# Re-timing three small visits in a fused attention and FFN kernel: a v product joined to its scores, a value pair moved ahead, and four k transposes given to the DMA queue

## The chip, the cores and the metric

The kernel runs on one core of one Trainium2 chip. The metric is device time in microseconds (us) of one execution, lower is better. Each timed comparison runs the changed kernel and the kernel before on the same chip, in rounds; ratios with 95% intervals come from those.

Before the change the median was 402.93 us (three runs, 402.53 to 404.41).

## The reference

```python
# 8 batches, 8 heads, 1024 positions, head size 64; E, F: 64 x 1024
k_proj = einsum('ks,bhsd->bhkd', E, k)
v_proj = einsum('ks,bhsd->bhkd', F, v)
attn   = softmax(q @ k_proj^T / sqrt(64))          # over 64 projected keys
x      = (attn @ v_proj), heads side by side        # 8192 x 512
h      = max(x @ w1, x @ w2, x @ w3)                # 512 -> 768, three times
out    = h @ w_out                                  # 768 -> 512
```

## The kernel before

The kernel does one batch of the FFN while it prepares the attention of the next one. TensorE (PE) works in program order. (A DMA *lands* when its data is complete at its destination.) The FFN products of batch b form a row of *steps*; a table, `plan(b)`, says which pieces of attention work ("visits") stand behind which step. Step `(ch, s)` is half `ch` of the batch; `s` from 0 to 5 are the up-projection steps (12 products of 128x512 each), 6 to 9 are output tiles (6 products each); `"mid"` means behind the eighth product of a step.

```python
# abridged; "..." marks cuts
def load(b, which):                       # q, k, v of one batch, 1 MiB each, POOL queue, cast to bf16
    for i in which:
        dma = nc.gpsimd.dma_start(out=tiles[i], in_=view((q, k, v)[i], b))
        if i == 0 and b - 1 in last_T:
            after(dma, last_T[b - 1])     # q of b waits for the DMA transpose of q of b-1

def qd(b, parts=1):                       # q: packed by DVE, turned by DMA into qTs[b]
    for lo in range(0, NPAIR, n):
        ...
        last_T[b] = nc.sync.dma_start_transpose(out=qTs[b][...], in_=q_p[...])

def kproj(b):                             # k product: 16 matmuls, then a copy to kps[b]
    ...
    copy("v", kps[b]..., t[:, 0:4 * D], ns, 0.43)

def kt(b):                                # k turned by PE: two transposes into PSUM, one DVE copy
    t, ns = two()
    for gg in range(2):
        nc.tensor.transpose(out=t[:, gg * P:(gg + 1) * P], in_=kps[b][:, gg, :], identity=ident)
    kpTs[b] = att.tile([P, NPAIR, KP], BF16, name="kpT")
    copy("v", kpTs[b]..., t[:, 0:2 * P]..., ns, 0.3)

def vproj(b): ...                         # v product: 16 matmuls, four copies to vps[b]
def sc(b, g, ...): ...                    # scores of head pair g: needs qTs[b] and kpTs[b]; then exp
def zc(b, queue): ...                     # softmax sums, their inverse, zd to DRAM, zi broadcast back
def vx(b, g): ...                         # attention values of pair g, scaled by zi into x

def plan(b):
    if b == 0:
        return {
            (0, 7): [qd(1, 2), ...],      # q of batch 1 is turned in two halves
            ...
            (1, 0): [kproj(1)],
            (1, 1): [kt(1)],
            (1, 2): [vproj(1), ld(2)],
            (1, (3, "mid")): [sc(1, 0, now=True), sc(1, 1)],
            (1, 4): [za(1, 0), sc(1, 2, now=True)],
            ...
        }
    ...
    if b == 2:
        return {
            (0, 2): [kproj(3), vproj(3), ld(4)],
            (0, 3): [kt(3)],
            (0, 4): [sc(3, 0, now=True), sc(3, 1)],
            ...
            (0, 7): [zc(3)],
            (0, 8): [qd(4)],
            (1, 3): [kproj(4), vproj(4), ld(5), vx(3, 0), vx(3, 1)],
            (1, 4): [kt(4)],
            (1, 7): [vx(3, 2), vx(3, 3), sc(4, 0)],
        }
    ...                                   # batches 3 and later: one general row of visits

# start of batch 0: FFN products and attention visits are interleaved one by one
(0, 1, 3): [lambda: v_pair(2), lambda: x(2)],
(0, 1, 5): [lambda: v_pair(3), ld(1)],
```

The softmax here doesn't subtract the row's maximum and nothing guards it: scores larger than these inputs give would overflow.

## Time and profile before

| | before |
|---|---|
| time, median | 402.93 us |
| span of the profiled run | 400.4 us |
| PE busy | 388.4 us, 97% |
| VectorE (DVE) / ScalarE (ACT) busy | 203.5 / 151.0 us |

These are lines of parts 1, 2 and 3 of the page of the kernel before. Part 1 gives busy us, share of the span and instructions; the line of digits gives the busy share of the 16 DMA engines in tenths, in 40 slices.

```profile
span 400.4 us, 5708 instructions
PE 388.4 (97%) x2244; PEld 176.7 (44%) x2286; DVE 203.5 (51%) x319; ACT 151.0 (38%) x242; POOL 34.2 (9%) x49
DMA  9999999968799998999989959990890229020202
q0 software_dynamic: 29104, 30.41, 47.0%
```

PE is the limit, at 97%. But the digits of the DMA engines are 9 in most slices up to 270 us: a landing may come just in time, and then a later one costs.

This is the list of waits of the kernel before, PE only: who waited, for whom, us in total, how many times, the longest.

```profile
PE banks L461 <- DVE warm_f L175: 1.5, 1, 1.5
PE banks L346 <- DMA v_t<-in_v_dram: 1.0, 1, 1.0
PE banks L490 <- DMA k_t<-in_k_dram: 0.9, 1, 0.9
PE banks L232 <- DVE vp L102: 0.7, 2, 0.5
```

These are four of its ten lines; the others come to 2.7 us, none of their waits over 0.3. The 1.0 us is the wait that step 1 of the change is after, and one of the two waits of L232 is what step 2 is after. There is little else.

The timeline of the kernel before around that wait, PE lines (start, us from start to end, engine, line, operation, tiles, shape, count, and in brackets the idle time before it and what ended it):

```profile
52.15 2.75 PE L583 MATMUL banks<-xT,w_sb 128*128 128x512 bf16 x12
55.95 1.06 PE L346 MATMUL banks<-v_t,efT 128*64 128x256 bf16 x16 [1.04 <-DMA v_t<-in_v_dram]
56.94 1.90 PE L583 MATMUL banks<-xT,w_sb 128*128 128x512 bf16 x8
58.77 0.63 PE L212 MATMUL banks<-qT,kpT 64*64 64x512 bf16 x8
59.33 3.63 PE L583 MATMUL banks<-xT,w_sb 128*128 128x512 bf16 x15
```

Twelve products start 0.216 us apart, so those from 52.15 make room at 54.74; the v product starts at 55.95. And the timeline of the kernel before around the q load of batch 4 and the first scores of batch 4 (`sc(4, 0)`):

```profile
131.20 0.88 POOL L201 DMA_DIRECT2D q_t<-in_q_dram  x1 [24.63 <-DMA qT<-q_p]
168.22 0.63 PE L232 MATMUL banks<-pT,vp 64*64 64x512 bf16 x8
168.71 0.41 PE L212 MATMUL banks<-qT,kpT 64*64 64x512 bf16 x4
169.22 0.88 POOL L201 DMA_DIRECT2D q_t<-in_q_dram  x1 [35.40 <-DMA qT<-q_p]
```

The scores (L212) start without a listed wait, but the transpose of q that they read landed at 168.67: the q load of batch 5, which waits for exactly that landing, is issued at 169.22.

### The profile page before, as it was taken

The numbers are of one execution on the slowest core, as the hardware profiler recorded it, in microseconds if no ns is written. First come the engines' busy times: TensorE is split into PE (matmuls) and PEld (weight loads), VectorE is DVE, ScalarE is ACT, GpSimd is POOL, SyncE is SP. The second block draws the span as 40 slices with busy tenths as digits, with TensorE's granted clock in tenths as the row PEclk, the third lists the DMA queues.
The fourth block names the chain that finished last, engine by engine and source line by source line (L and its number), as shares of the span: only waits on it lengthen the run. The fifth ranks groups of instructions, "written<-read, shape, count | busy, mean of one in ns | idle before, by whom it ended". The sixth has DMA issues, their size and how long they took to land.

```text
span 400.4 us, 5708 instructions
## 1 busy us (share of the span) xinstructions
PE 388.4 (97%) x2244; PEld 176.7 (44%) x2286; DVE 203.5 (51%) x319; ACT 151.0 (38%) x242; POOL 34.2 (9%) x49
## 2 busy tenths in 40 slices
PE   7999989999999999999999999999999999999996
PEld 3444443353444445444454445444454444444443
DVE  2348746762683525736274544744267342745251
ACT  2535428527222462253323532245323533132312
POOL 7440002000400200010020000100000000000000
PEclk9999999999999999999999999999999999999999
DMA  9999999968799998999989959990890229020202
GB/s 159 205 206 208 230 204 156 235 137 156 203 187 198 221 218 193 223 183 209 224 221 178 236 133 269 178 242 26 204 217 5 103 67 252 0 105 2 105 0 105
DMA packets 66330, 66.09 MB, mean 165 GB/s; under 512 B 30624, under 2 KB 58784, under 8 KB 66304
## 3 DMA queue, kind: packets, MB, share of 16 engines
q0 software_dynamic: 29104, 30.41, 47.0%
q1 hardware_dynamic: 37056, 35.20, 34.3%
q8 instruction: 17, 0.28, 0.3%
q10 hardware_dynamic: 144, 0.13, 0.1%
q14 instruction: 9, 0.07, 0.1%
HBM read 69.73 MB, written 16.97 MB: 217 GB/s over the span
## 4 chain that ended last, share of the span: by engine, by line
PE 84%; DMA 9%; DVE 2%; issue 2%; ACT 1%; POOL 0%; DVEq 0%; ACTq 0%; POOLq 0%
PE banks L583 56%; PE banks L687 18%; DMA v_t<-in_v_dram 8%; PE banks L346 3%; PE banks L232 2%; PE banks L212 2%; DMA k_t<-in_k_dram 2%; DVE xT L309 1%; PE banks L257 1%; ACT zi_all L298 1%; ACT zl L292 1%; PE banks L490 1%; DVE m L652 0%; PE banks L461 0%; PE banks L516 0%
## 5 line engine op out<-in xcount | busy, mean ns | idle before, releaser
L583 PE MATMUL banks<-xT,w_sb 128*128 128x512 bf16 x1119 | 254.8, 379 | 2.6 <-issue 0.8
L583 PEld LDWEIGHTS <-w_sb 128*128 128x128 bf16 x1152 | 109.9, 98 | 136.1 <-issue 8.5
L652 DVE TENSOR_TENSOR m<-banks,h1s 128x512 f32<-128x512 f32 x90 | 62.1, 690 | 135.3 <-ACT h1s L648 92.7
L648 ACT COPY h1s<-banks 128x512 f32<-128x512 f32 x90 | 52.6, 585 | 120.3 <-PE banks L583 118.8
L687 PE MATMUL banks<-wout_sb,hT 128*128 128x512 bf16 x370 | 85.6, 379 | 1.0 <-issue 0.8
L593 DVE TENSOR_TENSOR hT<-banks,m 128x512 bf16<-128x512 f32 x90 | 62.3, 692 | 9.3
L687 PEld LDWEIGHTS <-hT 128*128 128x128 bf16 x378 | 35.2, 98 | 47.4 <-issue 5.6
L102 ACT COPY o_sb<-banks 128x512 f32<-128x512 f32 (+1 forms) x56 | 32.6, 582 | 57.9 <-PE banks L687 57.6
L223 ACT ACTIVATE pT<-banks 128x1024 bf16<-128x1024 f32 (+1 forms) x36 | 32.8, 932 | 18.1 <-PE banks L212 18.1
L309 DVE TENSOR_TENSOR xT<-banks,zi_all 128x1024 bf16<-128x1024 f32 x28 | 33.1, 1219 | 11.7 <-PE banks L232 6.9
L201 POOL DMA_DIRECT2D q_t<-in_q_dram x7 | 6.1, 878 | 193.8 <-DMA qT<-q_p 118.8
L346 PEld LDWEIGHTS <-efT 128*64 128x64 bf16 x224 | 11.6, 110 | 4.5 <-issue 3.0
L102 DVE CAST vp<-banks 64x256 bf16<-64x256 f32 (+1 forms) x18 | 7.1, 397 | 12.5 <-ACT vp L102 9.5
L102 ACT CAST vp<-banks 64x256 bf16<-64x256 f32 x14 | 5.1, 364 | 21.4 <-PE banks L346 21.3
L232 PE MATMUL banks<-pT,vp 64*64 64x512 bf16 (+1 forms) x144 | 11.4, 364 | 0.7 <-DVE vp L102 0.7
L212 PE MATMUL banks<-qT,kpT 64*64 64x512 bf16 (+1 forms) x144 | 11.4, 362 | 0.4 <-DVE m L652 0.3
L292 ACT ACTIVATE zl<-banks 128x512 f32<-128x512 f32 (+1 forms) x12 | 8.9, 739 | 6.3 <-PE banks L232 5.3
L102 DVE COPY q_p<-q_t 128x1024 bf16<-128x1024 bf16 x28 | 10.4, 435 | 0.5 <-DMA q_t<-in_q_dram 0.5
L346 PE MATMUL banks<-v_t,efT 128*64 128x256 bf16 x112 | 7.3, 273 | 1.0 <-DMA v_t<-in_v_dram 1.0
L102 DVE COPY o_sb<-banks 128x512 f32<-128x512 f32 (+1 forms) x9 | 5.8, 653 | 4.5 <-PE banks L667 4.5
L346 PE MATMUL banks<-k_t,efT 128*64 128x256 bf16 x112 | 7.4, 276 | 0.0
L461 PE MATMUL banks<-warm_f 128*128 128x512 f32 x8 | 6.0, 895 | 1.5 <-DVE warm_f L175 1.5
(63 smaller groups left out, 120.9 us busy)
## 6 DMA issues: line engine op xcount, KB each, us to landing
out_dram<-o_sb SPq DMA_DIRECT2D x30, 512.0 KB, 4.6
zi_all<-zd SPq DMA_DIRECT2D x20, 512.0 KB, 8.0
q_t<-in_q_dram POOLq DMA_DIRECT2D x7, 1024.0 KB, 10.1
k_t<-in_k_dram POOLq DMA_DIRECT2D x7, 1024.0 KB, 16.4
v_t<-in_v_dram POOLq DMA_DIRECT2D x7, 1024.0 KB, 21.9
zi_all<-zd POOLq DMA_DIRECT2D x4, 512.0 KB, 7.6
w_sb<-in_moe_w_dram POOLq DMA_DIRECT2D x4, 384.0 KB, 11.1
k_t<-in_k_dram POOLq DMA_DIRECT2D x2, 512.0 KB, 8.7
```

What stands on the lines that cost most here:

```text
L102: done = {"v": nc.vector.tensor_copy, "s": nc.scalar.copy, "g": nc.gpsimd.tensor_copy}[eng](out=o, in_=i)
L212: nc.tensor.matmul(out=t[c * HALF:(c + 1) * HALF, hp, 0:n * P], lhsT=kpTs[b][rows, g, :], rhs=qTs[b][rows, at:at + n, :], start=True, stop ...
L223: nc.scalar.activation(out=pTs[b, g, lo], in_=t, func=AF.Exp, scale=scale)
L232: nc.tensor.matmul(out=t[hp * HALF:(hp + 1) * HALF, c, 0:nsi * HALF], lhsT=w(rows, hp), rhs=p[rows, hp, :], start=True, stop=True,)
L292: nc.scalar.activation(out=zl, in_=t, func=AF.Ln)
L309: nc.vector.tensor_tensor(out=xTs[b][:, g, lo:lo + nsi, :].rearrange("a (c s) p -> a c (s p)", c=2), in0=t, in1=zi, op=ALU.mult,)
L346: nc.tensor.matmul(out=t[hh * HALF:(hh + 1) * HALF, 0:width], lhsT=efT[:, si, (kv - 1) * KP:kv * KP], rhs=qkv[b][kv][:, heads[hh], si, :], ...
L583: nc.tensor.matmul(out=h, lhsT=w_sb[i][:, ct, jt * P:(jt + 1) * P], rhs=xTs[b][:, ct, ch * SPC:(ch + 1) * SPC, :], start=(ct == first), st ...
L593: nc.vector.tensor_tensor(out=o, in0=h, in1=other, op=ALU.max)
L648: nc.scalar.copy(out=h1s, in_=h[0][0])
L652: nc.vector.tensor_tensor(out=m12, in0=h[1][0], in1=h1s, op=ALU.max)
L687: nc.tensor.matmul(out=o_ps, lhsT=hTs[b, ch][:, jt, tt * P:(tt + 1) * P], rhs=wout_sb[:, jt, :], start=(jt == 0), stop=(jt == NJT - 1),)
```

## The change

Three steps, each meant to take a PE wait or PE work away.

1. Batch 1's v product moves from behind step (1, 2), where PE waits for its load, into the visit of batch 1's first scores.
2. Value pair 2 of batch 0 moves two FFN products ahead, so that these fill the time in which its values are copied.
3. k of batches 3, 5, 6 and 7 is turned by a DMA transpose on SP's queue rather than by PE. The next batch's q load is made to wait for it.

```diff
@@ load
             if i == 0 and b - 1 in last_T:
                 after(dma, last_T[b - 1])
+            if i == 0 and b - 1 in turned:
+                after(dma, turned[b - 1])
@@ new
+    def kd(b):
+        def f():
+            kpTs[b] = att.tile([P, 2, 2 * KP], BF16, name="kpT2")
+            turned[b] = nc.sync.dma_start_transpose(
+                out=kpTs[b], in_=kps[b].rearrange("a g x -> a (g x)")
+            )
+        return f
@@ plan(0)
-                (1, 2): [vproj(1), ld(2)],
-                (1, (3, "mid")): [sc(1, 0, now=True), sc(1, 1)],
+                (1, (3, "mid")): [sc(1, 0, now=True), sc(1, 1), vproj(1), ld(2)],
@@ plan(2)
-                (0, 2): [kproj(3), vproj(3), ld(4)],
-                (0, 3): [kt(3)],
+                (0, 2): [kproj(3), kd(3), vproj(3), ld(4)],
@@ plan(3 and later)
-            out[1, 2] = [kproj(n + 1), vproj(n + 1)] + out[1, 2]
-            out[1, 3] = [kt(n + 1)]
+            out[1, 2] = [kproj(n + 1), kd(n + 1), vproj(n + 1)] + out[1, 2]
@@ start of batch 0
-                    (0, 1, 3): [lambda: v_pair(2), lambda: x(2)],
+                    (0, 1, 1): [lambda: v_pair(2)],
+                    (0, 1, 3): [lambda: x(2)],
```

(The scores read the new layout of `kpT` where a batch was turned by DMA; `turned` starts empty; `ld(n + 2)` stands alone at step (1, 3) now that `kt` has gone from there.)

More of the change, by code (lines that the diff above doesn't have):

```diff
@@ L203, in load, with k_pair @@
                 after(dma, last_T[b - 1])
+            if i == 0 and b - 1 in turned:
+                after(dma, turned[b - 1])
+    def k_pair(b, g):
+        if b in turned:
+            return kpTs[b][:, g % 2, (g // 2) * KP:(g // 2 + 1) * KP]
+        return kpTs[b][:, g, :]
+    turned = {}
     def scores(b, g, lo, nsi):
@@ L213, in scores @@
                     out=t[c * HALF:(c + 1) * HALF, hp, 0:n * P],
-                    lhsT=kpTs[b][rows, g, :],
+                    lhsT=k_pair(b, g)[rows],
                     rhs=qTs[b][rows, at:at + n, :],
@@ L758, in plan @@
             out[0, 4] = [qd(n + 1)]
-            out[1, 2] = [kproj(n + 1), vproj(n + 1)] + out[1, 2]
-            out[1, 3] = [kt(n + 1)]
+            out[1, 2] = [kproj(n + 1), kd(n + 1), vproj(n + 1)] + out[1, 2]
             out[1, 6] += [sc(n + 1, 0)]
         if n + 2 < B:
-            out[1, 3] += [ld(n + 2)]
+            out[1, 3] = [ld(n + 2)]
         return out
```

## The prediction

> **What bounds it now.** TensorE. Page part 1: matmuls busy 388.4 of 400.4 us, clock 1.0. The list of PE waits sums to about 8 us, mostly at the start. A 128x512 product starts every 0.216 us (timeline; 12 take 2.59). So a step pays only if it removes PE work or ends a PE wait; DMA matters only where a landing comes after PE's need.
>
> **Step 1, v product of batch 1.** In the timeline the product starts at 55.95 although the FFN products before it allow 54.74: a gap of 1.2 us for v_t, issued 25.64, landed 55.90. Moved behind the first scores, it no longer waits. But those scores then come at about 56.4, and the first half of qT(1) (DMA transpose issued 43.95) landed only at 57.16. PE will wait about 0.8 us. The visit and the four products after it ended at 60.2; after: 57.3 + scores 0.56 + v product 0.99 + products 0.86 = 59.7. Worth 0.5 us, not 1.2.
>
> **Step 2, value pair 2.** v_t of that pair lands at 20.05. Before, its product starts at 20.19, vp is cast at 20.90 to 21.19, x starts at 21.25, PE idle 0.6 us. Two FFN products fill that gap, but they come from ahead of the value product, which now waits about 0.4 us: landing plus 1.2 us still sets x. Worth 0.05 us.
>
> **Step 3, k by DMA.** The two transposes cost PE only about 0.11 us a batch (timeline: 131.71 to 134.42 with 12 products, against 2.59). Four batches: -0.45 us. Added: a 64 KB transpose on SP's queue; the next q load waits for it. The Trainium skill, "DMA: Bandwidth & Descriptors", section "Issuing engines are not separate DMA queues", says all queues interleave on the same 16 engines; the trace agrees (512 KB outputs land in 2.6 us late in the run, in about 7 beside loads).
> - Batches 5, 6, 7: kpT has 4.5 us or more of slack, the delayed loads (2 to 5 us) 9 or more. Free.
> - Batch 3 is different. Loads of batch 4 started at 131.20, when qT(3) has landed. kp(3) is cast only at 131.36; the transpose stands behind two outputs that land at 131.86 and 133.16. So the loads start about 3 us later. To 169 the DMA is nearly full (mean share over 1): loads, zd, zi broadcasts, qT(4). qT(4) landed at 168.67 and the first scores of batch 4 start at 168.71: no slack. Idle DMA (151 to 153) absorbs about 1.5 us; I estimate qT(4) at 169.7 and a new PE wait of about 1.5 us, which eats the 0.6 us won so far and about 1 more.
>
> **Sum.** With the stall: 402.9 + 1.0 - 0.3 = 403.6. Without: about 402.0. Weighing both: 403.0 us, range 401.6 to 404.4. Faster over 2%: 0.01; within 2%: 0.97; slower over 2%: 0.02.
>
> **What shows it.** Right: no PE wait for v_t near 56, one of 0.5 to 1 for qT near 57; step 2 changes nothing after 21.5; q load of batch 4 issued near 133.7; qT(4) landing after 169.2 with a PE wait after it; no new PE waits from 180 on. Wrong: loads of batch 4 near 131, or qT(4) before 168.2: then 402.0 or below.
>
> **What would break it.** The k transpose overtaking the outputs; loads and broadcasts overlapping better than their engine time says; PSUM banks dealt anew (some tenths); spread between runs (402.5 to 404.4) as large as the effect.

## The result, and the profile after

The change made the kernel slightly slower: 403.93 us median (six runs, 403.34 to 405.0) against 402.78 (six runs of the kernel before, 402.1 to 404.41). The ratio is 1.0028, 95% interval 1.0005 to 1.0052. A ratio is the mean time of one kernel's fast runs over that of the other's of the same rounds, so it is not quite the ratio of the medians.

Page of the kernel after, parts 1 to 3, the same lines:

```profile
span 403.2 us, 5736 instructions
PE 392.3 (97%) x2278; PEld 176.7 (44%) x2278; DVE 202.8 (50%) x315; ACT 151.1 (37%) x242; POOL 34.3 (8%) x49
DMA  8999999988799699999997979598880229020202
q0 software_dynamic: 29104, 30.41, 47.0%
```

PE's busy time can't be compared to the microsecond (the trace of the kernel before lacks 33 of the 1152 products of the largest group), so the waits and the starts decide. The list of PE waits of the kernel after (five of its eight lines):

```profile
PE banks L221 <- DMA qT<-q_p: 1.9, 2, 1.5
PE banks L478 <- DVE warm_f L175: 1.5, 1, 1.5
PE banks L355 <- DMA k_t<-in_k_dram: 1.4, 1, 1.4
PE banks L507 <- DMA k_t<-in_k_dram: 1.3, 1, 1.3
PE banks L241 <- DVE vp L102: 0.2, 1, 0.2
```

The wait for v_t and one wait for vp are gone. In their place stand two waits for qT, 1.9 us together. The timeline of the kernel after shows the first where step 1 was made:

```profile
50.53 1.06 PE L355 MATMUL banks<-k_t,efT 128*64 128x256 bf16 x16 [1.43 <-DMA k_t<-in_k_dram]
54.24 4.48 PE L600 MATMUL banks<-xT,w_sb 128*128 128x512 bf16 x20
59.14 0.63 PE L221 MATMUL banks<-qT,kpT 64*64 64x512 bf16 x8 [0.41 <-DMA qT<-q_p]
59.69 1.06 PE L355 MATMUL banks<-v_t,efT 128*64 128x256 bf16 x16
```

The scores now come first and wait for the first half of qT(1). The second wait is at batch 4. First the k transpose of batch 3 on SP's queue and the q load that waits for it, then the scores:

```profile
132.76 1.17 SPq L456 DMA_TRANSPOSE kpT<-kp  x1
135.64 0.88 POOL L201 DMA_DIRECT2D q_t<-in_q_dram  x1 [27.72 <-DMA kpT<-kp]
169.47 0.63 PE L241 MATMUL banks<-pT,vp 64*64 64x512 bf16 x8
171.59 0.41 PE L221 MATMUL banks<-qT,kpT 64*64 64x512 bf16 x4 [1.49 <-DMA qT<-q_p]
172.11 0.88 POOL L201 DMA_DIRECT2D q_t<-in_q_dram  x1 [33.84 <-DMA qT<-q_p]
```

The most useful reading is a list of where PE stands in the program, kernel by kernel. This table is worked out from the traces: the start of one weight load of the up-projections, minus that of the same load in the trace of the kernel before. (74.27 is the start of batch 1's FFN.) A column that steps up has lost time between two rows, one that steps down has won it.

```
PE's place, us later (+) or earlier (-) than in the trace of the kernel before
at, in before     after  k3_alone  k567_alone  all_but_k3  held_load
 17.35  start     +0.84     +0.00       -0.08       +0.89      +0.32
 45.55            +0.59     +0.20       -0.04       +0.45      +0.31
 74.27            +1.36     +0.51       +0.39       +0.14      +0.29
131.70            +1.36     +0.51       +0.39       +0.14      +0.29
146.89            +1.25     +0.40       +0.39       +0.15      +0.29
171.44            +2.88     +0.94       +0.34       +0.09      +1.52
204.21            +2.89     +0.94       +0.34       +0.09      +1.52
217.95            +2.78     +0.94       +0.23       -0.02      +1.52
264.47            +2.67     +0.94       +0.12       -0.13      +1.52
310.98            +2.56     +0.95       +0.01       -0.24      +1.53
383.76            +2.56     +0.95       +0.01       -0.23      +1.53
end, 400.40       +2.82     +0.88       +0.30       +0.07      +1.51
```

In the column of the kernel after:

- It is 0.84 us late before anything changed has run: the loads of batch 0 landed late, the second q load at 11.87 us against 11.04. (Over all fourteen traces the start of the FFN follows that landing by 6.31 to 6.37 us; the very first q load is no guide: in s2_alone it landed at 6.50 as before, and PE started 0.42 us late.) This is chance, and the profiled run (405.0 us) is the slowest of its six. So the 2.8 us between the two spans is not the cost of the change.
- It loses 1.63 us between 146.89 and 171.44, around the wait for qT(4).
- It wins 0.11 us where a transpose visit was taken from PE, four times (146.89, 217.95, 264.47, 310.98).
- It loses 0.26 us after PE's work is over.

### The profile page after: what moved, and what is told of

Its sections match the earlier page's. It is cut to its first block, busy times and chain, and to the rows that moved or that the text cites. A ratio compares the mean times of both kernels' runs of the same rounds, so it can differ in the third digit from the quotient of the medians.

```text
span 403.2 us, 5736 instructions
## 1 busy us (share of the span) xinstructions
PE 392.3 (97%) x2278; PEld 176.7 (44%) x2278; DVE 202.8 (50%) x315; ACT 151.1 (37%) x242; POOL 34.3 (8%) x49
## 4 chain that ended last, share of the span: by engine, by line
PE 82%; DMA 15%; ACT 1%; DVE 1%; issue 0%; POOL 0%; DVEq 0%; ACTq 0%; POOLq 0%
PE banks L600 54%; PE banks L704 18%; DMA qT<-q_p 7%; DMA k_t<-in_k_dram 7%; PE banks L355 3%; PE banks L241 2%; PE banks L221 2%; PE banks L266 1%; DVE xT L318 1%; ACT zi_all L307 1%; ACT zl L301 1%; PE banks L507 1%; PE banks L478 0%; PE banks L533 0%; PE banks L684 0%
## 5 line engine op out<-in xcount | busy, mean ns | idle before, releaser
L704 PE MATMUL banks<-wout_sb,hT 128*128 128x512 bf16 x378 | 86.9, 380 | 0.1
L221 PEld LDWEIGHTS <-kpT 64*64 64x64 bf16 x144 | 4.0, 105 | 9.1 <-issue 7.2
```

What stands on the lines that cost most here:

```text
L221: nc.tensor.matmul(out=t[c * HALF:(c + 1) * HALF, hp, 0:n * P], lhsT=k_pair(b, g)[rows], rhs=qTs[b][rows, at:at + n, :], start=True, stop= ...
L704: nc.tensor.matmul(out=o_ps, lhsT=hTs[b, ch][:, jt, tt * P:(tt + 1) * P], rhs=wout_sb[:, jt, :], start=(jt == 0), stop=(jt == NJT - 1),)
```

## The experiments

The theory: all that the change lost is at the first scores of batch 4. The q load of batch 4 is held until the k transpose of batch 3 has landed; the DMA engines are full from there to qT(4); qT(4) had no slack. Rivals: the loss is spread over the DMA turns (their own DMA work, their place on SP's queue), or lies in the re-dealt PSUM banks, or is chance.

### k of batch 3 alone, and k of batches 5 to 7 alone

```diff
 k3_alone: the kernel before, with
-                (0, 2): [kproj(3), vproj(3), ld(4)],
-                (0, 3): [kt(3)],
+                (0, 2): [kproj(3), kd(3), vproj(3), ld(4)],
 k567_alone: the kernel before, with
-            out[1, 2] = [kproj(n + 1), vproj(n + 1)] + out[1, 2]
-            out[1, 3] = [kt(n + 1)]
+            out[1, 2] = [kproj(n + 1), kd(n + 1), vproj(n + 1)] + out[1, 2]
```

Both keep the wait of the next q load on the k transpose. They were run on another chip.

> The kernel before with only batch 3's k turned by DMA, the wait of the next q load on it included. My theory (the wait holds back the loads of batch 4, so qT(4) lands late): q load of batch 4 issued about 4 us later than before relative to qT(3)'s landing, qT(4) about 1.5 us later, a PE wait of about 1.4 us before the first scores of batch 4; time +1.4 us against before. Rival (the loss of the whole change is spread over all DMA turns, or is start jitter and re-dealt PSUM banks): within 0.4 us of before, and no PE wait for qT near 170.

Measured: 404.09 us against 402.69, ratio 1.0043 (1.0028 to 1.0059). Batch 3 alone costs as much as the whole change, or more (the intervals overlap). The q load of batch 4 came 3.49 us after qT(3)'s landing (before: 0.54). In its one trace, which was the fastest of its six runs, the wait for qT(4) was only 0.4 us:

```profile
PE banks L221 <- DMA qT<-q_p: 0.4, 1, 0.4
```

So the place is as expected, while the size in that trace is smaller than in the timed mean. The next runs are needed to show that this wait is the cost.

> The kernel before with only k of batches 5, 6 and 7 turned by DMA. My theory: no new PE wait, each removed PE visit is worth 0.11 us, time -0.3 us against before. Rival (every DMA turn costs because of its DMA work and the held loads): +0.5 us or more, with PE waits after 200 us.

Measured: 402.86 us against 402.69, ratio 1.0009 (0.9992 to 1.0026). The expected gain is not there. The time alone does not exclude the rival's 0.5 us, but the PE waits after 200 us that it named are not in the trace. The table shows why the gain is missing. The three removed visits are worth 0.11 us each to PE, as expected (0.34, 0.23, 0.12, 0.01). But the end of the program came 0.29 us later relative to PE's last work. That is taken up under "the end of the program" below.

### The whole change without batch 3, and without the wait

```diff
 all_but_k3: the kernel after, with
-                (0, 2): [kproj(3), kd(3), vproj(3), ld(4)],
+                (0, 2): [kproj(3), vproj(3), ld(4)],
+                (0, 3): [kt(3)],
 after_no_wait: the kernel after, with
-            if i == 0 and b - 1 in turned:
-                after(dma, turned[b - 1])
```

The wait guards no data: the q load and the k transpose share no tile. The result was correct. The Trainium skill, "DMA: Bandwidth & Descriptors", section "Rules for kernel authors", says that a DMA transpose beside ordinary DMAs needs no ordering; this run agrees.

> The whole change, but k of batch 3 turned by PE as before. My theory: step 1 gives 0.5, step 2 up to 0.2, batches 5 to 7 give 0.3, nothing is lost: -0.8 to -1.0 us against before, no PE wait for qT near 170. Rival (the loss lies in the other steps): as slow as the whole change, +1 us.

Measured (five runs): 402.25 us against 402.69, ratio 0.9992 (0.9977 to 1.0007). Taking batch 3 out removes the loss: from 1.0028 to 0.9992 is 0.36%, or 1.45 us. The gain that I expected of the rest (0.8 to 1.0 us) is not clear of noise.

> The whole change, without the wait of the q loads on the k transposes (no data passes between them). My theory: the q load of batch 4 is issued at qT(3)'s landing + 0.6 us as before, so qT(4) is in time; -0.8 to -1.1 us against before. If instead the DMA work of the k transpose or its place on the SP queue is the cause: still about +1 us, with the PE wait for qT near 170 unchanged. If the k transpose among the loads lands late, a new PE wait for kpT stands before the scores of batch 3 (near 137).

Measured: 402.91 us against 402.69, ratio 1.0019 (0.9992 to 1.0045, six runs from 402.41 to 406.21; the slowest, at clock 0.995, pulls the mean up, and the medians differ by 0.2 us). The q load went out 0.54 us after qT(3), and the wait at batch 4 was gone. But the case that I had named last came true as well. The timeline of that kernel:

```profile
131.05 0.88 POOL L201 DMA_DIRECT2D q_t<-in_q_dram  x1 [24.52 <-DVE hT L608]
131.36 1.17 SPq L454 DMA_TRANSPOSE kpT<-kp  x1
137.94 0.63 PE L219 MATMUL banks<-qT,kpT 64*64 64x512 bf16 x8 [0.92 <-DMA kpT<-kp]
```

The same 64 KB transpose that lands in 2.3 us when the loads are held (132.76 to 135.07 in the kernel after) takes 6.5 us beside them (131.36 to 137.89), and PE waits for kpT instead. The Trainium skill, "DMA: Bandwidth & Descriptors", section "Issuing engines are not separate DMA queues", says that what SP and POOL issue shares the same engines; the trace agrees with these two numbers. So for batch 3 there is a choice of two waits: with the ordering qT(4) is late, without it kpT(3) is.

### The held load alone, without any DMA turn of k

```diff
 before_held_load: the kernel before, with
             if i == 0 and b - 1 in last_T:
                 after(dma, last_T[b - 1])
+            if i == 0 and b == 4:
+                after(dma, outs[-1])      # the last output of batch 1
```

This is the cleanest test: the delay without its reason. It was run on another chip.

> The kernel before, k turned by PE throughout; only the q load of batch 4 is held until batch 1's last output has landed, about 2.5 us after qT(3). If the held load is the cause of batch 3's loss, qT(4) lands 0.5 to 1.5 us later after qT(3) than before and PE waits for it near 170: +0.7 to +1.5 us. If the DMA transpose itself or its place on the SP queue were the cause, this kernel is as fast as before.

Measured: 404.06 us against 402.94, ratio 1.0028 (1.0012 to 1.0043): the very ratio of the change. The load went out at 134.03, 3.06 us after qT(3); qT(4) landed 39.21 us after qT(3) (before: 38.02). The timeline of that kernel at batch 4 (the bracket of the load names a DVE copy that had ended at 133.75; the load was held for batch 1's last output, which landed at 133.47, and such a load goes out about 0.55 us after the landing):

```profile
134.03 0.88 POOL L201 DMA_DIRECT2D q_t<-in_q_dram  x1 [27.18 <-DVE vp L102]
168.52 0.63 PE L234 MATMUL banks<-pT,vp 64*64 64x512 bf16 x8
170.23 0.41 PE L214 MATMUL banks<-qT,kpT 64*64 64x512 bf16 x4 [1.09 <-DMA qT<-q_p]
```

PE lost 1.2 us there (+0.29 to +1.52 in the table). k is turned by PE throughout, so neither the DMA work of a k transpose nor its place on SP's queue is needed for the loss. The held load suffices.

How the delay travels can be read from all fourteen traces. k and v of batch 4 stand behind the held q load. In the ten traces with the load not held, v of batch 4 had landed 0.6 to 2.0 us before the DMA transpose of q of batch 4 was issued; in the four with it held, v landed 1.2 to 1.8 us after that issue, so loads and transpose met in the DMA engines. (From 152 to 154 us the engines' packets filled 0.50 of their time in the kernel before and 1.24 in this one; over 1 means that packets overlap.) The size differs much from trace to trace: qT(4) landed 37.1 to 38.7 us after qT(3) where the load was not held (mean 38.0) and 38.3 to 39.5 where it was (mean 38.9). So about 1.0 us is the better figure for the delay than the 1.52 us of the single pair before and after.

### Steps 1 and 2 alone, and the v product first

```diff
 s1_alone: the kernel before, with
-                (1, 2): [vproj(1), ld(2)],
-                (1, (3, "mid")): [sc(1, 0, now=True), sc(1, 1)],
+                (1, (3, "mid")): [sc(1, 0, now=True), sc(1, 1), vproj(1), ld(2)],
 s1_v_first: instead
+                (1, (3, "mid")): [vproj(1), ld(2), sc(1, 0, now=True), sc(1, 1)],
 s2_alone: the kernel before, with
-                    (0, 1, 3): [lambda: v_pair(2), lambda: x(2)],
+                    (0, 1, 1): [lambda: v_pair(2)],
+                    (0, 1, 3): [lambda: x(2)],
```

> The kernel before with step 1 alone (v product of batch 1 behind the first scores, in one visit). In the traces so far PE reaches batch 1's FFN second half at the landing of v(1) + 18.37 us where the v product comes first by itself, and at the landing of qT(1)'s first half + 16.53 us where the scores come first, and that half lands about 1.1 us after v(1). So: 0.7 us faster than before, with a PE wait for qT near 57 instead of the one for v_t. Rival (the wait for v_t was worth its full 1.2 us): 1.2 us faster and no wait for qT.

(The place meant is the start of batch 1's FFN, not its second half.) Measured: 402.8 us against 402.94, ratio 0.9993 (0.9976 to 1.0009). The timeline of that kernel shows the exchange of one wait for another:

```profile
52.30 4.48 PE L583 MATMUL banks<-xT,w_sb 128*128 128x512 bf16 x20
57.53 0.63 PE L212 MATMUL banks<-qT,kpT 64*64 64x512 bf16 x8 [0.75 <-DMA qT<-q_p]
58.09 1.06 PE L346 MATMUL banks<-v_t,efT 128*64 128x256 bf16 x16
```

Measured from its own start, PE was 0.38 us ahead by 74 us (0.24 ahead in place, 0.14 late at the start). Then it gave 0.31 us back before 171 us: it came earlier to the scores of batch 4, and qT(4), landed at 168.74, did not. Less than the 0.7 us expected is left, and it isn't clear of noise.

> As step 1 alone, but the v product stands ahead of the scores in the visit, so it fills the time in which qT(1)'s first half is still on its way. If the wait for qT(1) is what step 1 left, it shrinks to 0.3 us or less, and the time is 1.2 us below before, 0.5 us below step 1 alone. If something else binds there (vp's copies, PSUM banks), no better than step 1 alone.

Measured: 401.5 us against 402.94, ratio 0.9964 (0.9947 to 0.9981). The timeline of that kernel:

```profile
53.07 4.48 PE L583 MATMUL banks<-xT,w_sb 128*128 128x512 bf16 x20
57.48 1.06 PE L346 MATMUL banks<-v_t,efT 128*64 128x256 bf16 x16
58.48 0.63 PE L212 MATMUL banks<-qT,kpT 64*64 64x512 bf16 x8
```

Neither the v product nor the scores wait: v(1) had landed at 56.99, and the half of qT(1) at 58.15, while PE did the v product. The order within one visit decides: first the work whose data comes first. From the landing of qT(1)'s first half to the start of batch 1's FFN PE needed 15.85 us here, 16.53 in s1_alone. That trace difference is 0.7 us; the timed one between the two kernels, 1.3 us, is larger, and single traces do not show where the rest is.

> The kernel before with step 2 alone. It may gain 0.05 to 0.4 us by 28 us into the run, but PE then waits for v(1), whose landing the DMA sets, so nothing of it is left after 60 us: within 0.2 us of before. Rival: the gain stays, 0.2 to 0.4 us faster.

Measured: 402.99 us against 402.94, ratio 1.0001 (0.9981 to 1.002). In that trace step 2 won nothing even at first (PE 0.42 us late at the start, 0.53 at 45.55), and at 74.27 it was 1.10 us late: it waited 1.5 us for v(1), which landed at 57.00. In all six traces with the old order of step 1, PE reached 74.27's place 18.37 to 18.38 us after v(1)'s landing. So what PE wins before 50 us is paid back there.

### The end of the program

In k567_alone the end moved by 0.29 us although PE did not. At the end SP passes through the DMA semaphores in a fixed order, about 0.06 us each. The DMAs issued by SP and ACT take eight semaphores in turn, so the number of such DMAs decides which one the last output gets (read from the order of SP's waits at the end; the five counts below fit it). In k567_alone it got 110, and SP had yet to pass six more after it:

```
last output's semaphore, from its landing to the end of the program (all fourteen traces)
DMAs from SP and ACT   semaphore   us            kernels
71                     117         0.97 - 0.99   before, s1_alone, s1_v_first, s2_alone, before_held_load
72                     118         0.93          k3_alone
74                     110         1.28 - 1.29   k567_alone, all_but_k3
75                     113         1.21 - 1.23   after, after_no_wait, after_sc4_later
80                     118         0.91 - 0.97   the three with split outputs, below
```

The test adds six DMAs and no other work: the outputs of batches 6 and 7 are written one tile at a time. It was run on another chip.

```diff
 k567_split_out: k567_alone, with
-        if b == B - 1 and ch == NCHUNK - 1:
+        if b >= 6:
             nc.sync.dma_start(out=ov[:, si], in_=o_sb[:, tt % 2])
```

> k of batches 5, 6 and 7 turned by DMA as in k567_alone, and the outputs of batches 6 and 7 written in single tiles: six more DMAs, no other work. In k567_alone PE was 0.33 us ahead by batch 6, but after the last landing the program needed 1.28 us to end against 0.99 before: SP walks through the DMA semaphores in a fixed order, and the three DMAs more had moved the last output from the last but one semaphore (117) to an earlier one (110). Nine DMAs more in all bring it to the last one (118). If that is the cause, last landing to end takes 0.9 to 1.0 us, and the time is 0.3 to 0.4 us below before. Rival (the end is just noise, or the DMA turns cost something): the end stays at 1.25 us or more, or varies, and the time is that of before.

Measured: 402.3 us against 403.12, ratio 0.9989 (0.9969 to 1.0009). The end took 0.93 us, on semaphore 118, as expected. The gain in time has the expected size and isn't clear of noise. That the position in the order sets the length of the end is shown by the traces; that it is worth 0.3 us of time is seen in the spans, not in the timed ratio alone.

### Versions that the runs point to

```diff
 v_first_k567_split: k567_split_out, with the visit of s1_v_first
 v_first_k567_sc4_later: the same, and
-                (1, 7): [vx(3, 2), vx(3, 3), sc(4, 0)],
+                (1, 7): [vx(3, 2), vx(3, 3)],
+                (1, 8): [sc(4, 0)],
 after_sc4_later: the kernel after, with that last edit only
```

> The version that the experiments point to: the v product of batch 1 ahead of the scores in their visit (1.2 to 1.4 us), k of batches 5, 6 and 7 by DMA (0.33 us), outputs of batches 6 and 7 in single tiles for the place of the last semaphore (0.05 us), batch 3 by PE, step 2 left out. If the parts add up: 1.5 to 1.8 us below before, PE waits for neither v_t, qT nor kpT after 50 us. If PE, being early, meets qT(4) at 168 (slack 0), up to 0.5 us of it is lost there.

Measured: 401.75 us against 403.12, ratio 0.9963 (0.9945 to 0.998): a gain, of 1.4 to 1.5 us, but no larger than that of s1_v_first alone. In its trace PE stepped back by 0.29 us at batch 4, where qT(4) landed at 168.99.

> The whole change, k of batch 3 by DMA with its wait included; only the first scores of batch 4 stand one step later (one output tile, 1.3 us of PE work, more lies between). If those scores' wait for qT(4) is where the change lost its time, the wait shrinks from 1.5 to about 0.2 us and the time is about 1.3 us below the whole change, 0 to 0.5 us below before. If it was lost elsewhere, it stays at +1.1 us over before.

Measured: 402.38 us against 402.87, ratio 0.9994 (0.9974 to 1.0014). It was run on another chip. With the one visit moved, and k of batch 3 still turned by DMA and its load still held (q load 3.67 us after qT(3)), the loss of the change no longer shows. (It was not timed against the change itself, and the two intervals overlap a little: 1.0005 to 1.0052 for the change.) The timeline at batch 4:

```profile
168.02 0.63 PE L241 MATMUL banks<-pT,vp 64*64 64x512 bf16 x8
168.58 1.47 PE L704 MATMUL banks<-wout_sb,hT 128*128 128x512 bf16 x6
169.98 0.41 PE L221 MATMUL banks<-qT,kpT 64*64 64x512 bf16 x4
```

qT(4) landed at 169.16, an output tile is done meanwhile, and the scores at 169.98 wait for nothing. This, with the held load, settles the cause: adding the delay alone makes the loss, clear of noise, and with the waiting visit moved alone the wait is gone from the trace and the loss from the time.

> The version v_first_k567_split with the first scores of batch 4 one step later. There PE lost 0.3 us to qT(4) in its trace; with 1.3 us of slack that wait is gone: no PE wait for qT near 170 and 0.2 to 0.4 us faster than that version, 1.6 to 1.9 us below before. If the re-ordered scores cost as much as the wait (banks held longer), no gain.

Measured: 401.68 us against 402.87, ratio 0.997 (0.9955 to 0.9985), with no PE wait for v_t, qT or kpT after 50 us. It is clearly faster than the kernel before. It is not to be told apart from s1_v_first or v_first_k567_split: PE still gave back 0.18 us around 171 without a listed wait. It gave back the same 0.18 us (-0.21 to -0.03) in after_sc4_later, so this goes with the moved visit; why isn't shown. The simplest of the faster versions is s1_v_first: one line in another place.

## Why the prediction was right or wrong

The time (403.0 said, 403.93 measured, range 401.6 to 404.4) and the class (within 2%) were right. But the range holds the case with the stall and the case without, so the time alone could not have told the mechanism right from wrong; and against the kernel before, 0.1 us of loss was said and 1.1 measured. The points below decide (its list of PE waits, by the way, sums to 6.8 us, not 8):

- **Step 1, "worth 0.5 us, not 1.2"**: the mechanism was right. The wait for v_t went and one for the first half of qT(1) came (0.41 us in the kernel after, 0.75 in s1_alone). PE's gain in s1_alone's trace was 0.38 us, and 0.31 of it was lost again at qT(4). The timed gain is 0.07% and not clear of noise.
- **Step 2, "worth 0.05 us"**: the time agrees (1.0001). In the trace of the kernel after, PE did win 0.24 us by 22 us (0.84 late at the start, 0.60 then), so "changes nothing after 21.5" was wrong there. It won nothing for another reason than I gave: a later landing, v(1)'s or qT(1)'s, sets the pace.
- **Step 3, 0.11 us per batch**: exact, in every trace where PE did not wait for the turned k.
- **Batches 5, 6, 7, "free"**: true for PE. I missed the end of the program, where three or four DMAs more cost 0.29 or 0.22 us through the order of the semaphores (of the 0.26 us in the table). That is most of what the three visits win.
- **Batch 3**: the load held 3 us (3.09 us later after qT(3) than before: 3.63 against 0.54), half of it absorbed (qT(4) 39.54 us after qT(3) against 38.02, so 1.52 late), a PE wait of 1.5 us (1.49). The place and the mechanism were right; that the wait agrees to 0.01 us is luck. The prediction made it of a landing about 1.0 us late and 0.6 us that PE had won; in the trace they were 1.52 and 0.11. The absolute landing, 169.7 in the prediction and 171.55 in the trace, is off by 1.85, of which 1.36 is that PE and DMA were already late for the reason below.
- **The sum**: the prediction gave 403.6 for the case with the stall and 402.0 for the case without, and mixed them to 403.0. The stall came, and the measured 403.93 lies next to the first number. How near says little: the sum had about 1.6 us of loss at batch 3 and 0.9 us of gain elsewhere, and timed alone batch 3 cost 0.43% (1.7 us), while steps 1 and 2 and batches 5 to 7 showed no gain clear of noise. No term of the sum had the end of the program.
- **"No new PE waits from 180 on"**: right.
- **What was not foreseen**: the early part is paced by landings that vary from run to run. Over the fourteen traces PE starts the FFN between 17.27 and 18.24 us, k(1) lands between 47.76 and 50.49, and PE waits up to 1.5 us for it in some traces and not at all in others. The trace of the kernel before happened to be an early one. In the six traces with the old order of step 1, PE's place at 74.27 differs by 1.1 us for this reason. Traces exist of single runs only, so that the spread of the timed runs comes from there is likely, but not shown.

The runs of the single parts add up, by their ratios, to +0.5% (1.0043, 1.0009, 0.9993, 1.0001), the whole change measures +0.28%; each has an interval of about 0.15% or more either way, so this is no contradiction, and no proof of additivity either.

## What to carry to other kernels

Before moving work to a queue that "has time", look for the landing with no slack further down: the list of waits shows only waits that happened, so compare landing times with the first use of the data (here 168.67 and 168.71). An ordering put between two DMAs delays everything that stands behind the second one, and a full DMA stretch carries that delay tens of microseconds to the next use without slack; here the cure was to move that use, not the DMA. Within one visit, put first the work whose data lands first.

## What the Trainium skill lacked or had wrong

- **End of the program** (no page that I found has it): after the last DMA has landed, SP passes through the DMA semaphores in a fixed order, about 0.06 us each. Depending on the semaphore that the last output gets, the end took 0.91 to 1.29 us in these traces. Adding DMAs anywhere in the program can shift it by 0.3 us.
- **Rate of DMA transposes** ("Advanced Engine Details and Errata", section "X-Bar Transpose (TRN2)"): the page says that they are as fast as regular DMAs and expects 350 to 400 GB/s. Here a whole q of a batch (1 MiB, from SBUF to SBUF) took 6.7 to 22.8 us from issue to landing in the kernel before. The fastest, of batch 2, was the only DMA at work from 82.2 to 87.3 us: in that time it moved 0.98 MB in packets of 256 bytes, 193 GB/s, or 218 GB/s up to 86.7 us, until when the DMA engines were busy throughout. No run here tries another shape.
- **Cost of a small DMA beside loads** ("DMA: Bandwidth & Descriptors", section "Issuing engines are not separate DMA queues"): the page says that the queues interleave, but not by how much a small transfer suffers. The 64 KB transpose of batch 3's k took 2.3 us from issue to landing with the loads held and 6.5 us beside them.
